# Second layer of an attention and two-FFN kernel: a larger room, a value's parts a stage later, banks in turn at two stages, one high part later

## The chip, the cores and the metric

The kernel runs on one core of a Trainium2 chip. The metric is device time in microseconds of one execution; times shown are medians of several. A profiled execution gives the trace that is quoted below. Engines are named as in the profile: PE is TensorE's matmuls, PEld its weight loads, DVE VectorE, ACT ScalarE, POOL GpSimd, SP SyncE, whose queue issues the loads and stores.

## The reference

What is computed, cut to what matters here: a thresholded attention, a gated layer, and a second layer whose activation is a square in the middle, zero below and the value itself above.

```python
def _moe_ref(x, w_gate, w_val, w_out):          # x: 2304 x 512, d_ff 1536
    gate = 1.0 / (1.0 + np.exp(-(x @ w_gate)))
    val = x @ w_val
    return (gate * val @ w_out).astype(np.float32)

def _moe2_ref(x, w_in, w_out):                  # d_ff 2048
    h = x @ w_in
    g = np.where(h >= 1, h, np.where(h <= -1, 0.0, (h + 1) ** 2 / 4.0))
    return (g @ w_out).astype(np.float32)

def reference(**kwargs):
    attn_out = _attn_ref(...)                   # 4 batches, 8 heads, 576 x 64
    x = attn_out.transpose(0, 2, 1, 3).reshape(2304, 512)
    return _moe2_ref(_moe_ref(x, ...), ...)
```

## The kernel before, in words

All matmuls are made of 32-bit floats split into a high and a low part: `hi` is ACT's copy of a value into the matmul's input type, `lo` is DVE's difference of the value and `hi`, and three matmuls (high by high, low by high, high by low) stand for one. So every operand of a matmul costs ACT one copy and DVE one difference, its "parts".

The program has three stretches. Attention comes first (to about 270 us), then most of the first layer. What the change touches is the third, from about 578 us: the last ten blocks of the first layer's last pass, and the second layer. Tokens are worked in three passes of 768 (`T`). The up-projection of two blocks of 128 hidden columns for one pass is a *stage*, `stage(g)`. It computes a two-by-two block product with seven products instead of eight: `product(i, ps)` issues six matmuls of 128x384 into one of two PSUM banks, `ps[0]` and `ps[1]`, and the table `PRODUCTS` says which. Products 0, 2, 4 and 6 use `ps[0]`, products 1, 3 and 5 `ps[1]`. ACT evacuates products 0 and 2 (`s1`, line 787, and `u2`, line 796), DVE makes five sums from the others (`add`, line 762), among them `u3`, which is the tile `high`. Their results are the two values `c[0]` and `c[1]` of the stage.

Stages 0 to 9 (`g` below `N1` = 10, `q = g - N1` negative) belong to the first layer, in pairs: an even stage gives two gates, an odd one the two values that are multiplied with them (`gated_steps`: the product on DVE, the high part on ACT, the low part on DVE). Stages 10 to 33 (`q` from 0 to 23) are the second layer, eight to a pass; `j` is the place in the pass, so stages 10, 18 and 26 are the first of a pass (`j` = 0), and 11, 19 and 27 the second. `value_steps` makes the activation there in four steps: the square on ACT (lines 683 and 684), the choice on DVE (690), the high part `hh` on ACT (692), the low part `hl` on DVE (693). `i` is 0 for a stage's first value and 1 for its second one.

Behind stage `g` TensorE issues output matmuls: `down` in the first layer (line 871), `down_pair(q - 1, y)` in the second (line 853), 36 matmuls of 128x512, 18 for the first value of the stage before and 18 for the second. After stages 0 and 8 none are issued; the lengths in `lens` say so with a 7.

The order on ACT and DVE is planned by hand-set due times. `due(first, last, steps)` puts a chain of steps on a list; each step has a time, an estimated cost on DVE and on ACT, and a mark that says whether it may stand between products (`small`). `fill(slot, room, act)` issues what is due: all whose `last` slot has come, and in order of time whatever still fits into the room. A stage has slots `4g` to `4g + 3`; the last one, behind its seven products, has the large room:

```python
                    room = lens[g] - 6.6 - (3 if j == 0 else 0)
                fill(4 * g + 3, room, room)
```

Between products, `fill(4 * g + 1, 2.6 if q == 0 else 1.5, 1.3, small=True)` stands behind product 1 and its sum, and small ones behind the later sums. The same list holds the parts of the weights (`split_steps`, lines 728 and 729: `win` for the next stage's products, `wout` for an output), the weights' differences (`w_sums`, line 633, into `tsum`), and the parts of the tokens for the next pass (`xflat`, `xmore`). Engines work their own queues in the order in which the program issues to them; SP loads weights (`load_pair`, `load_sums`) when the slots they go into are free. At a pass's second stage `store` copies the six finished output banks and issues their stores.

Of the kernel before, what the change touches and what calls it, by code (L numbers as in the profile page):

```python
# [13 lines left out]
AF = mybir.ActivationFunctionType  # L14
# [9 lines left out]
def f32(ap):  # L24

    return ap.bitcast(F32)
# [3 lines left out]
def kernel(  # L30
# [17 lines left out]
    nc = tc.nc  # L48
# [436 lines left out]
    def ffn(att):  # L485


        with ExitStack() as st:
# [170 lines left out]
            def load_sums(q):  # L659
                nc.sync.dma_start(out=tsum, in_=tsaved[q % NQ])  # L660
# [18 lines left out]
            def value_steps(c, r, h, at):  # L679


                def square():
                    nc.scalar.activation(r, c, AF.Relu, scale=0.5, bias=half)
                    nc.scalar.activation(r, r, AF.Square)

                return [
                    (at[0], 0, 1.6, False, square),
                    (
                        at[1], 0.84, 0, False,
                        lambda: nc.vector.scalar_tensor_tensor(c, c, 1.0, r, op0=ALU.max, op1=ALU.min),  # L690
                    ),
                    (at[2], 0, 0.72, False, lambda: nc.scalar.activation(h[0], c, AF.Copy)),
                    (at[3], 0.84, 0, True, lambda: nc.vector.tensor_tensor(h[1], c, f32(h[0]), op=ALU.subtract)),  # L693
                ]
# [5 lines left out]
            lens = [7] + [11] * (N1 - 3) + [7, 15] + [15] * (NPASS * NQ + 1)  # L700
            start = lambda g: sum(lens[:g])

            def due(first, last, steps):
                waiting.append((steps[0][0], len(order) + len(waiting), first, last, steps))
                waiting.sort(key=lambda x: x[:2])
# [33 lines left out]
            def due_w(g):  # L739
                at = start(g)  # L740
                sums = g < N1 + NQ
                if sums and g:
                    due(4 * g - 3, 4 * g - 1, [(at - 3 + 0.1 * i, 0.4, 0, True, w) for i, w in enumerate(w_sums(g))])
                for i, (when, first, last, cost) in enumerate(
                    ((-3.2 if sums else -1, 4 * g - 3, 4 * g - 1, 0.6), (1.3, 4 * g - 1, 4 * g + 1, 0.32), (1, 4 * g - 1, 4 * g - 1, 1.1))
                ):
                    due(first, last, split_steps(at + when, cost, cost - 0.1, *w_split(g, i)))

            def stage(g):

                q = g - N1
                n = q + N1 // 2 if q >= 0 else g // 2
                ps = [ps_a.tile([P, 512], F32, tag=f"a{i}", name="pu")[:, :HT] for i in range(2)]
                if q >= 0:
                    c = [(vals[:, 0], sqs[:, 1])[q % 2], (vals[:, 1], rbs, early_raw[1])[q % 3][:, :T]]
                elif g % 2 == 0:
                    c = cs[n] = [(sqs, vals)[n % 2][:, i] for i in range(2)]
                else:
                    c = [x[:, :T] for x in (rbs, early_raw[1])]
                s1, u2 = (hp_.tile([P, HT], F32, tag="act", name="act") for _ in range(2))  # L760
                u3 = high0[:, :HT]
                add = lambda o, a, b: nc.vector.tensor_tensor(o, a, b, op=ALU.add)  # L762
                t0, t1 = slice(0, HT), slice(HT, T)
                more, j = g + 1 < N1 + NPASS * NQ, (q % NQ if q >= 0 else g + NQ - N1)
                last, o = j == NQ - 1, (q // NQ + 1 if q >= 0 else 0)
                if more:
                    due_w(g + 1)
                if j == NQ - 4 and o < NPASS:
                    for i, w in enumerate(x_sums(o + 1)):
                        at = start(g + 1) + 8 * (i + 1) * lens[g] / 15  # L770
                        due(4 * g, 4 * (g + 3) - 1, [(at, 0.84, 0, True, w)])
                if last and more:
                    due_x(o + 1)
                for i in range(2):
                    if q >= 0:
                        first, end, at = 4 * g, 4 * g + 5, start(g + 1) + 5.2 + 0.3 * i
                        src = w32[q][i][:, KD * P : 2 * KD * P]
                    elif g % 2:
                        break
                    else:  # L780
                        f = F0 + 2 * n + i
                        wsp[0, NPASS - 1, f] = (None, None, *wout(n, i))
                        src = w32[0, NPASS - 1, f][:, 2 * KD * P :]
                        first, end, at = 4 * g, 4 * g + 7, start(g + 1) + 2 + 9 * i
                    due(first, end, split_steps(at, 0.6, 0.5, *wout(n, i), src))
                product(0, ps)
                nc.scalar.activation(s1, ps[0], AF.Copy)  # L787
                product(1, ps)
                add(c[0][:, t0], ps[1], s1)
                fill(4 * g + 1, 2.6 if q == 0 else 1.5, 1.3, small=True)  # L790
                if q + 1 >= NQ and more:
                    load_sums(q + 1)
                if q + 2 >= 0 and q + 2 < NPASS * NQ:
                    load_pair(q + 2)
                product(2, ps)
                nc.scalar.activation(u2, ps[0], AF.Copy)  # L796
                if lens[g] > 7 and q != 0:
                    fill(4 * g + 2, 0, 2.2, small=True, begin=True)
                product(3, ps)
                add(u3, ps[1], u2)  # L800
                fill(4 * g + 2, 0.45, 0, small=True)
                product(4, ps)
                add(c[1][:, t1], ps[0], u3)
                fill(4 * g + 2, 0.45, 0, small=True)
                product(5, ps)
                add(c[0][:, t1], ps[1], u2)
                fill(4 * g + 2, 0.45, 0, small=True)
                product(6, ps)
                add(c[1][:, t0], ps[0], u2)
                at = start(g + 1)  # L810
                if q < 0:
                    if g % 2 == 0:
                        sig = lambda x: nc.scalar.activation(x, x, AF.Sigmoid)
                        due(4 * g + 3, 4 * g + 7, [(at + 1.6 + i, 0, 0.9, True, lambda x=x: sig(x)) for i, x in enumerate(c)])
                    else:
                        for i in range(2):
                            h = hts[0, NPASS - 1, F0 + 2 * n + i] = h_tiles()
                            when = ((1.2, 1.3, 1.5), (1.25, 1.4, 1.7))[i]
                            if q == -1:
                                when = ((3.9, 4.2, 4.3), (6.5, 6.6, 7))[i]  # L820
                            due(4 * g + 3, 4 * g + 7, gated_steps(c[i], cs[n][i], h, [at + x for x in when]))
                    room = lens[g] - (4.6 if q == -1 else 5.6)
                else:
                    h = hts[q] = [h_tiles(), h_tiles()]
                    at += 7
                    for i in range(2):
                        r = vals[:, 1] if i and not more else sqs[:, 0]
                        if not more:
                            when = ((-6, -4, -3.8, -3.6), (-5, -3, -2.8, -2.6))[i]
                        elif last:  # L830
                            when = ((-2.5, -2.4, -2.2, -2), (1, 1.2, 1.4, 1.6))[i]
                        else:
                            when = ((-6.2, -6.15, -5.9, -5.5), (-5.4, -5.3, -5.2, -5.1))[i]
                        due(4 * g + 3, 4 * g + 7, value_steps(c[i], r, h[i], [at + x for x in when]))
                    room = lens[g] - 6.6 - (3 if j == 0 else 0)
                fill(4 * g + 3, room, room)

            def gated_steps(c, s, h, at):

                return [  # L840
                    (at[0], 0.92, 0, True, lambda: nc.vector.tensor_tensor(c, c, s, op=ALU.mult)),
                    (at[1], 0, 0.82, True, lambda: nc.scalar.activation(h[0], c, AF.Copy)),
                    (at[2], 0.92, 0, True, lambda: nc.vector.tensor_tensor(h[1], c, f32(h[0]), op=ALU.subtract)),
                ]

# [67 lines left out]
            early, taken, xops, begun, cs = {}, [], {}, [], {}  # L913
# [40 lines left out]
            n = 3 * KD * P  # L954
# [4 lines left out]
            for s in range(NB):  # L959
# [19 lines left out]
                if order[s][:2] == (0, 1) and later:  # L979
                    p, i, normalise = later.pop(0)  # L980
# [18 lines left out]
            for g in range(N1 + NPASS * NQ):  # L999
                q = g - N1  # L1000
# [3 lines left out]
                if q == -2:  # L1004
                    n = 2 * KD * P
# [3 lines left out]
                if q <= 0 < g != N1 - 2:  # L1009
                    n = NB - 2 + g  # L1010
# [61 lines left out]
```

## Time and profile before

| | |
|---|---|
| median of 3 runs | 1096.84 us (1093.95 to 1098.01) |
| the profiled execution | 1097.53 us, of which the span of its instructions is 1095.7 us |
| PE busy | 1075.7 us, 98% of the span |
| DVE busy | 898.3 us, 82% |
| ACT busy | 632.7 us, 58% |
| mean granted clock of TensorE | 0.995 of full |

The busy time of an engine is its share over stretches with different limits. For a change at single places, what counts is which engine waits there, for what, and how long; the chain that ended last and the timeline tell that.

### The profile page before, as it was taken

Reading aid. Unit: us, or ns where it says so; the run is one execution under the profiler, and the core shown is the slowest. Engines: PE = TensorE matmul, PEld = TensorE weight load, DVE = VectorE, ACT = ScalarE, POOL = GpSimd, SP = SyncE. Lnnn points to the kernel's source line nnn. Section 1 sums busy time; section 2 is a strip of 40 time slices with the busy share of each in tenths; the row PEclk is TensorE's granted clock in tenths of the full one; section 3 lists DMA queues with packets and bytes.
Section 4 is the critical chain, followed back from the end, with each engine's and each line's share of the span. In section 5 each row is a group of like instructions: output and inputs, shape, how many; then the busy total and the mean of one; then the engine's idle time right before and its main releaser. Section 6 shows DMA issues by size and latency. Waiting matters only on the chain.

```text
span 1095.7 us, 18519 instructions
## 1 busy us (share of the span) xinstructions
PE 1075.7 (98%) x6930; PEld 924.2 (84%) x6930; DVE 898.3 (82%) x1591; ACT 632.7 (58%) x1024; POOL 148.6 (14%) x311
## 2 busy tenths in 40 slices
PE   8999999999999999999999999999999999999998
PEld 6666666667999999999999999889888899889887
DVE  7999999997999999888797778977877667776663
ACT  6888888886434344333354544565566565665653
POOL 4556666562000000000000000000000000000000
PEclk9999999999999999999999999999999999999999
DMA  5344344514665566565541111222234322233301
GB/s 158 69 101 80 91 101 96 108 33 124 232 231 177 173 223 231 183 228 196 199 183 50 66 68 39 88 106 96 79 119 169 116 68 106 96 135 116 115 21 58
DMA packets 62842, 134.97 MB, mean 123 GB/s; under 512 B 9360, under 2 KB 35616, under 8 KB 62752
## 3 DMA queue, kind: packets, MB, share of 16 engines
q1 hardware_dynamic: 62608, 133.49, 38.1%
q8 instruction: 54, 0.88, 0.3%
q14 instruction: 36, 0.29, 0.1%
q10 hardware_dynamic: 144, 0.29, 0.1%
HBM read 106.96 MB, written 26.81 MB: 122 GB/s over the span
## 4 chain that ended last, share of the span: by engine, by line
PE 88%; ACT 5%; DVE 5%; issue 2%; POOL 0%; DVEq 0%; POOLq 0%
PE pu L674 22%; PE y L853 17%; PE y L871 13%; PE pgv L522 6%; PE pgv L521 6%; PE pgv L523 6%; PE av L339 6%; PE w L253 5%; PE w L307 4%; ACT ex L275 2%; PE w L250 1%; ACT xall L349 1%; DVE s L263 1%; DVE xflat L729 0%; ACT rl L325 0%
## 5 line engine op out<-in xcount | busy, mean ns | idle before, releaser
L853 PE MATMUL y<-wout,hh 128*128 128x512 f32 x576 | 186.3, 398 | 0.0
L674 PE MATMUL pu<-xflat,win 128*128 128x384 f32 x816 | 159.8, 337 | 1.8 <-DVE sqs L762 1.3
L674 PEld LDWEIGHTS pu<-xflat,win 128*128 128x128 f32 x816 | 143.5, 188 | 6.5 <-DVE sqs L762 2.3
L871 PE MATMUL y<-hh,wout 128*128 128x512 f32 (+1 forms) x576 | 146.2, 336 | 0.0
L522 PE MATMUL pgv<-xflat,win 128*128 128x384 f32 x400 | 133.9, 335 | 0.4 <-DVE xflat L514 0.4
L521 PE MATMUL pgv<-xflat,win 128*128 128x384 f32 x400 | 133.8, 335 | 0.0
L523 PE MATMUL pgv<-xflat,win 128*128 128x384 f32 x400 | 133.7, 334 | 0.0
L853 PEld LDWEIGHTS y<-wout,hh 128*128 128x128 f32 x576 | 109.6, 190 | 24.9
L674 PE MATMUL pu<-xmore,win 128*128 128x384 f32 x612 | 123.8, 336 | 1.4 <-ACT act L796 0.8
L263 DVE TENSOR_SCALAR_CACHE_REDUCE s<-w,nscale 128x576 f32<-128x576 f32 x144 | 112.4, 812 | 9.2 <-PE w L253 7.2
L853 PE MATMUL y<-wout,hl 128*128 128x512 f32 x288 | 115.2, 400 | 3.8 <-DVE hl L693 3.8
L283 DVE SCALAR_TENSOR_TENSOR p<-s,mx,ex 128x576 f32<-128x576 f32 x144 | 111.6, 808 | 0.0
L674 PEld LDWEIGHTS pu<-xmore,win 128*128 128x128 f32 x612 | 107.7, 188 | 3.4 <-ACT act L787 2.3
L275 ACT ACTIVATE ex<-s,mx 128x576 f32<-128x576 f32 x144 | 104.3, 766 | 6.2 <-DVE s L263 5.8
L871 PEld LDWEIGHTS y<-hh,wout 128*128 128x128 f32 x576 | 98.0, 188 | 11.3
L871 PE MATMUL y<-hl,wout 128*128 128x512 f32 (+1 forms) x288 | 97.1, 337 | 0.0
L266 POOL TENSOR_SCALAR mx<-mx,tau_b 128x1 f32<-128x1 f32 x144 | 87.5, 607 | 54.9 <-DVE s L263 54.6
L253 PE MATMUL w<-qk 64*128 64x288 f32 x512 | 89.9, 439 | 2.7 <-DVE s L263 2.7
L315 ACT ACTIVATE r<-w 128x1024 f32<-128x1024 f32 x64 | 65.2, 1018 | 30.3 <-PE w L307 29.9
L575 ACT ACTIVATE hh<-act 128x384 fp32r<-128x384 f32 x52 | 27.3, 524 | 93.0 <-DVE act L572 93.0
L253 PEld LDWEIGHTS w<-qk 64*128 64x128 f32 x512 | 50.8, 191 | 33.7 <-DVE s L263 18.4
L339 PE MATMUL av<-r,v 128*64 128x320 f32 (+1 forms) x512 | 75.8, 418 | 1.8 <-ACT xall L349 1.1
(164 smaller groups left out, 1903.8 us busy)
## 6 DMA issues: line engine op xcount, KB each, us to landing
words<-in_moe_w_out_dram SPq DMA_DIRECT2D x26, 512.0 KB
w<-saved SPq DMA_DIRECT2D x24, 512.0 KB
wmore<-saved SPq DMA_DIRECT2D x24, 512.0 KB
w<-saved SPq DMA_DIRECT2D x14, 768.0 KB
words<-in_moe_w_in_dram SPq DMA_DIRECT2D x16, 512.0 KB
saved<-w SPq DMA_DIRECT2D x16, 512.0 KB
tsum<-tsaved SPq DMA_DIRECT2D x16, 512.0 KB
wmore<-saved SPq DMA_DIRECT2D x10, 768.0 KB
```

Source lines behind the costliest of these rows:

```text
L253: nc.tensor.matmul(w[:, s, :HS], t[es, 0, u * P : u * P + P], t[es, 1, c], start=True, stop=True)
L263: nc.vector.tensor_scalar(t[:, e], w[:, :, :HS], nscale, None, op0=ALU.mult, op1=ALU.min, accum_out=mx[:, 0, e : e + 1])
L266: nc.gpsimd.tensor_scalar(mx[:, 1, e : e + 1], mx[:, 0, e : e + 1], tau_b, None, op0=ALU.add)
L275: nc.scalar.activation(ex[:, e], t[:, e], AF.Exp, scale=-1.0, bias=mx[:, 0, e : e + 1])
L283: nc.vector.scalar_tensor_tensor(pr[:, e], t[:, e].rearrange("p a b -> p (a b)"), mx[:, 1, e : e + 1], ex[:, e].rearrange("p a b -> p (a b ...
L339: nc.tensor.matmul(av[e * D : e * D + D, :n], vs[p % 3][:, e, c], rt[r][:, e, c] if c < nf else rl[r], start=c == 0, stop=c == nf,)
L521: nc.tensor.matmul(ps, ih[:, i, kk], xh, start=(kk == 0), stop=False)
L522: nc.tensor.matmul(ps, ih[:, i, kk], xl, start=False, stop=False)
L523: nc.tensor.matmul(ps, il[:, i, kk], xh, start=False, stop=(kk == KD - 1))
L674: nc.tensor.matmul(ps[bank], l[:, k], r[:, k], start=bool(new) and k == m == 0, stop=k == HK - 1 and m == 2, skip_group_check=True,)
L853: nc.tensor.matmul(y[b], l[:, ts_], r, start=first and m == 0, stop=last and m == 2)
L871: nc.tensor.matmul(at(y, a, b), l[:, ds_], r[:, c], start=new and m == 0, stop=last and m == 2, skip_group_check=True,)
```

## The change

Four edits, all in `stage` and in the steps it plans:

- Behind a stage of length 7 (so in stages 1 and 9) the two banks change roles.
- In stage 9 (`q == -1`) the high part of the second gated value is no longer marked as small, so it may not stand between products.
- In a pass's second stage (`j` = 1) the high and the low part of the second value get a chain of their own, which is due in the last slot of the stage behind.
- In a pass's first stage (`j` = 0) the last slot's room is reduced by 2 instead of 3.

```diff
@@ -751,6 +751,8 @@
                 q = g - N1
                 n = q + N1 // 2 if q >= 0 else g // 2
                 ps = [ps_a.tile([P, 512], F32, tag=f"a{i}", name="pu")[:, :HT] for i in range(2)]
+                if g and lens[g - 1] == 7:
+                    ps.reverse()
                 if q >= 0:
@@ -818,7 +820,7 @@
                             if q == -1:
                                 when = ((3.9, 4.2, 4.3), (6.5, 6.6, 7))[i]
-                            due(4 * g + 3, 4 * g + 7, gated_steps(c[i], cs[n][i], h, [at + x for x in when]))
+                            due(4 * g + 3, 4 * g + 7, gated_steps(c[i], cs[n][i], h, [at + x for x in when], q < -1 or i == 0))
                     room = lens[g] - (4.6 if q == -1 else 5.6)
@@ -831,15 +833,19 @@
-                        due(4 * g + 3, 4 * g + 7, value_steps(c[i], r, h[i], [at + x for x in when]))
-                    room = lens[g] - 6.6 - (3 if j == 0 else 0)
+                        steps = value_steps(c[i], r, h[i], [at + x for x in when])
+                        if j == i == 1:
+                            due(4 * g + 7, 4 * g + 7, steps[2:])
+                            steps = steps[:2]
+                        due(4 * g + 3, 4 * g + 7, steps)
+                    room = lens[g] - 6.6 - (2 if j == 0 else 0)
                 fill(4 * g + 3, room, room)
 
-            def gated_steps(c, s, h, at):
+            def gated_steps(c, s, h, at, small=True):
 
                 return [
                     (at[0], 0.92, 0, True, lambda: nc.vector.tensor_tensor(c, c, s, op=ALU.mult)),
-                    (at[1], 0, 0.82, True, lambda: nc.scalar.activation(h[0], c, AF.Copy)),
+                    (at[1], 0, 0.82, small, lambda: nc.scalar.activation(h[0], c, AF.Copy)),
```

The matmuls and their order stay as they are, apart from the banks of stages 1 and 9. ACT and DVE issue the same instructions in another order at four places: in stages 10 to 12, and at the ends of stages 18 and 26, which are alike. Three are shown, first before, then after; line numbers behind the first edit are larger by 2 to 8 in the changed kernel.

On DVE, the end of stage 18, the first of the second pass: the choice for the first value of the stage, the last weight parts for stage 19, the copies of three finished output banks (before L894, after L900), and the first sum of stage 19.

```order
L690 SCALAR_TENSOR_TENSOR vals<-vals,sqs 128x768
L729 TENSOR_TENSOR win_3507<-tsum,win_89 128x1024
L729 TENSOR_TENSOR win_3507<-w_2_84,win_89 128x256
L894 COPY xall<-y_3730 128x512
L894 COPY xall<-y_3732 128x512
L894 COPY xall<-y_3734 128x2x256
L762 TENSOR_TENSOR sqs<-pu,act 128x384
```

```order
L690 SCALAR_TENSOR_TENSOR vals<-vals,sqs 128x768
L729 TENSOR_TENSOR win_3507<-tsum,win_89 128x1024
L729 TENSOR_TENSOR win_3507<-w_2_84,win_89 128x256
L693 TENSOR_TENSOR hl<-vals,hh 128x768
L900 COPY xall<-y_3730 128x512
L900 COPY xall<-y_3732 128x512
L900 COPY xall<-y_3734 128x2x256
L764 TENSOR_TENSOR sqs<-pu,act 128x384
```

The low part of stage 18's first value now stands ahead of the copies; before, it stood behind stage 19's sums and a `wout` part. ACT's high part moves with it, from between stage 19's products to ahead of the last `win` part here.

On ACT, stage 10, the first of the second layer: the evacuation of product 0 (L787, after L789), that of product 2 (L796, after L798), the high part of stage 9's second gated value (`raw_88`, L842, after L848), and weight parts (L728).

```order
L787 ACTIVATE act<-pu 128x384
L842 ACTIVATE hh<-raw_88 128x768
L796 ACTIVATE act<-pu 128x384
L728 ACTIVATE win_89<-wmore 128x512
L683 ACTIVATE sqs<-vals,half 128x768
```

```order
L789 ACTIVATE act<-pu 128x384
L728 ACTIVATE win_89<-wmore 128x512
L728 ACTIVATE wout_3508<-w_1_83 128x512
L798 ACTIVATE act<-pu 128x384
L848 ACTIVATE hh<-raw_88 128x768
L683 ACTIVATE sqs<-vals,half 128x768
```

The high part has moved behind both evacuations, and two weight parts stand in its place. DVE's low part of that value moves behind the stage's five sums in the same way, a weight part takes its place there, and the second value's square and choice (L683, L684, L690) come into stage 10's end from stage 11's.

On ACT, from the end of stage 11, the second of the first pass, into stage 12: the square of stage 11's second value (`rb`), its high part (L692), and stage 12's evacuations of products 0 and 2.

```order
L683 ACTIVATE sqs<-rb,half 128x768
L684 ACTIVATE sqs<-sqs 128x768
L692 ACTIVATE hh<-rb 128x768
L787 ACTIVATE act<-pu 128x384
L728 ACTIVATE win_89<-w_1_83 128x512
L728 ACTIVATE wout_3508<-wmore 128x512
L796 ACTIVATE act<-pu 128x384
L728 ACTIVATE wout_6156<-w_0_82 128x512
```

```order
L683 ACTIVATE sqs<-rb,half 128x768
L684 ACTIVATE sqs<-sqs 128x768
L789 ACTIVATE act<-pu 128x384
L728 ACTIVATE win_89<-w_1_83 128x512
L728 ACTIVATE wout_3508<-wmore 128x512
L798 ACTIVATE act<-pu 128x384
L728 ACTIVATE wout_6156<-w_0_82 128x512
L692 ACTIVATE hh<-rb 128x768
```

The high part has moved behind stage 12's evacuations, and DVE's low part of it behind stage 12's sums.

## Rows read from the trace of the kernel before

**Rows 1.** Chain that ended last, second layer: start us, us, engine, line, count.

```profile
582.33 7.33 PE pu L674 x42
...
597.94 4.19 PE y L871 x24
...
840.24 7.38 PE pu L674 x42
849.72 9.88 PE y L853 x35
859.60 7.32 PE pu L674 x42
866.92 8.40 PE y L853 x36
...
979.58 9.86 PE y L853 x35
```

**Rows 2.** List of waits, PE: waited for; us in total, times, longest.

```profile
PE y L853 <- DVE hl L693: 3.8, 2, 1.9
```

**Rows 3.** Windows: us, busy PE PEld DVE ACT POOL, PEclk, DMA share, GB/s.

```profile
849.70:853.70 4.00, 3.98 (x11) 3.15 (x12) 2.35 (x3) 3.10 (x4) 0.00 (x0) 0.58 0.00 0
...
979.50:983.50 4.00, 3.92 (x10) 3.11 (x11) 2.35 (x4) 3.04 (x4) 0.00 (x0) 0.57 0.00 0
```

**Rows 4.** Timeline behind stage 19 and in stage 20, DVE and ACT: start, us.

```profile
848.72 0.95 DVE L693 TENSOR_TENSOR hl<-vals,hh 128x768 fp32r<-128x768 f32 x1
849.59 0.95 DVE L690 SCALAR_TENSOR_TENSOR raw<-raw,sqs 128x768 f32<-128x768 f32 x1
...
850.57 0.84 ACT L692 ACTIVATE hh<-raw 128x768 fp32r<-128x768 f32 x1 [3.70 <-DVE raw L690]
...
851.45 0.96 DVE L693 TENSOR_TENSOR hl<-raw,hh 128x768 fp32r<-128x768 f32 x1 [0.91 <-ACT hh L692]
...
861.79 0.56 DVE L762 TENSOR_TENSOR vals<-pu,act 128x384 f32<-128x384 f32 x1 [3.20 <-PE pu L674]
```

**Rows 5.** Timeline in stage 9, DVE.

```profile
680.47 0.95 DVE L611 TENSOR_TENSOR xall<-xall 128x768 f32<-128x768 f32 x1
681.93 0.56 DVE L762 TENSOR_TENSOR rb<-pu,act 128x384 f32<-128x384 f32 x1 [0.52 <-PE pu L674]
```

**Rows 6.** Timeline in stage 10, DVE and weight loads.

```profile
698.65 0.94 DVE L841 TENSOR_TENSOR raw<-raw,sqs 128x768 f32<-128x768 f32 x1
...
700.50 0.96 DVE L843 TENSOR_TENSOR hl<-raw,hh 128x768 fp32r<-128x768 f32 x1 [0.91 <-ACT hh L842]
...
700.90 1.00 PEld L674 LDWEIGHTS pu<-xmore,win 128*128 128x128 f32 x6 [1.12 <-ACT act L796]
...
701.72 0.55 DVE L762 TENSOR_TENSOR high<-pu,act 128x384 f32<-128x384 f32 x1
...
702.32 1.00 PEld L674 LDWEIGHTS pu<-xflat,win 128*128 128x128 f32 x6 [0.42 <-DVE high L762]
```

**Rows 7.** Groups by form, DVE, 700 to 760 us: busy us, mean ns.

```profile
L633 DVE TENSOR_TENSOR tsum<-wmore,tsum 128x256 f32<-128x256 f32 x5 | 2.1, 418 | 0.0
...
L729 DVE TENSOR_TENSOR win<-wmore,win 128x512 fp32r<-128x512 f32 x3 | 2.0, 681 | 0.0
```

**Rows 8.** Timeline in stage 12, ACT and weight loads.

```profile
729.92 0.85 ACT L692 ACTIVATE hh<-rb 128x768 fp32r<-128x768 f32 x1 [1.02 <-DVE rb L690]
...
731.19 0.99 PEld L674 LDWEIGHTS pu<-xmore,win 128*128 128x128 f32 x6 [0.76 <-ACT act L787]
...
732.88 0.99 PEld L674 LDWEIGHTS pu<-xflat,win 128*128 128x128 f32 x6 [0.69 <-DVE vals L762]
```

**Rows 9.** Windows of 1 us behind stage 19, columns as in rows 3.

```profile
849.00:850.00 1.00, 0.28 (x1) 0.28 (x2) 1.00 (x2) 0.00 (x0) 0.00 (x0) 1.00 0.02 8
```

**Rows 10.** Timeline behind stage 19, the parts of `tsum`.

```profile
853.02 1.04 ACT L728 ACTIVATE win<-tsum 128x1024 fp32r<-128x1024 f32 x1
...
854.10 1.23 DVE L729 TENSOR_TENSOR win<-tsum,win 128x1024 fp32r<-128x1024 f32 x1
```

## Prediction

> **What bounds the kernel now.** I read the chain that ended last first. In the second layer it is TensorE almost without a break: a stage of seven products takes 7.32 us, the 36 output matmuls behind it 8.40 us, and the next stage follows at once [rows 1]. So only a place where that chain is broken can give time back, and I looked for breaks by the starts of pieces: a stage that starts later than the end of the piece before it, or a piece that is too long for its count. Six places in reach of the change show one. The largest are in the second stage of the second and of the third pass: the seven products that start at 840.24 end at 847.62, the output matmuls go on at 849.72 and then need 9.88 us for 35, where 36 took 8.40 [rows 1]. The list of waits names the reason for the gap: `y` waited for `hl` of line 693, twice, 1.9 us the longest [rows 2]. The windows of these stretches show the rest: right behind each gap TensorE's granted clock is 0.58 and 0.57, a mixture of its two levels of 1.2 and 2.4 GHz, for some 4 us [rows 3]. Before the fall TensorE had idled; nothing else is different there.
>
> **The two pass starts (first value's parts before the stores).** In the order of before, the low part of the first value stands behind the next stage's seven products, two sums and a `wout` part: it runs at 848.72 and ends at 849.67 [rows 4], and the second matmul of the output waits for it. With the larger room it runs at the end of the first stage, some 9.5 us earlier, ahead of the copies of the stored tile. The DVE work is the same, one instruction of 0.95 us there and not here. From the start of the output (847.62) to the next stage (859.60) are 11.98 us; undisturbed it is 8.40 [rows 1]. The difference of 3.58 us is the stall and the slow clock together, and the second such place has the same piece, 9.86 us for 35 at 979.58 [rows 1]. Two of them: 7.16 us.
>
> What is late next? The second value's low part. Its chain at the same place is line 690 (849.59), the ACT copy (850.57), and line 693 (851.45, ended 852.41) [rows 4]. Without the first low part in front, all three come 0.87 us earlier (849.59 less 848.72), and the low part is ready at 851.54. The output reaches it after 18 of its 36 matmuls, at 847.62 + 4.20 = 851.82, and the low one is the second there. So it is in time by some 0.3 us, no more. The stage after that starts 3.6 us earlier than now; DVE idled 3.20 us before its first sum there (861.79, [rows 4]) and gains the 0.87, so it keeps pace with 0.5 us to spare. The copies of the stored tile begin 0.87 us later; nothing overwrites those banks until the next output, over 5 us on.
>
> **Banks in turn at two stages.** Stages 1 and 9 follow a stage without output matmuls between. Stages 0 and 1 take 15.61 us (582.33 to 597.94), two undisturbed stages 14.64 [rows 1]: 0.97 us lost, because product 0 writes the bank that product 6 just filled and DVE still reads. With the banks exchanged it writes the one freed a product earlier, and product 1 comes to the busy bank a product later, when that sum is over. I take 0.97 for stage 1. In stage 9 DVE stands in the way: the x sum (680.47) runs in front of the first sum, which idled 0.52 us for TensorE before 681.93 [rows 5]; it can come only that much earlier, and product 3 needs it. I take 0.52. The bound from below for both is 0, if DVE, full in the stages behind, starts its own chain no earlier; the bound from above is 0.97 each.
>
> The list of waits would give less for these places. It counts the idle time of matmuls, and the Trainium skill ("Perfetto Trace Analysis", "Identifying the Most-Contended Engine") says that matmul busy time misleads and the weight loads' is to be looked at. By matmul idle time the pass starts would be worth the 3.8 us of that row, not 7.16; the chain's starts and ends side with the skill.
>
> **One high part later (stage 10).** ACT copied the second gated value ahead of the evacuation of product 2, and waited with it for DVE's product at 698.65. So product 4 waited 1.12 us for that evacuation, and DVE waited 0.91 us for the copy before its low part at 700.50; the sum `high`, for which product 5 waits, ran at 701.72 [rows 6]. Afterwards a weight part of 512 and two differences of 256 stand there on DVE in place of the low part. By their means, 0.68 and 0.42 [rows 7], the sum starts at 698.65 + 0.94 + 0.68 + 2 x 0.42 = 701.11 or a little earlier. The evacuation no longer ends it, DVE does. Gain 0.6 to 0.7; I take 0.65. Bounds: 0, if another wait takes the place, and 1.54 (1.12 and the 0.42 that product 5 waits, [rows 6]). The value's own parts are needed only after 24 output matmuls, some 4 us after the stage, and come about 2 us before.
>
> **Second value's parts a stage later.** By the order it changes the first pass alone: at the other two the parts stood behind the next stage already. In stage 12 the weight loads of product 2 waited 0.76 us for the evacuation of product 0 and those of product 3 then 0.69 us for a sum; ACT's copy of that value, at 729.92, and DVE's low part behind it stood in front [rows 8]. Both go behind the stage's products, so 1.45 us at most; a little of it is caught up in the loads, and I take 1.4. It moves two instructions of 0.85 and 0.96 us to the end of stage 12, where the output needs them only after 18 matmuls (4.2 us). Two `wout` parts now run a stage later, so the load into their slot is issued some 6 us later on SP; that slot is read a stage on.
>
> **Sum.** 7.16 + 0.97 + 0.52 + 0.65 + 1.4 = 10.7 us. From the profiled execution's 1097.53 us that gives 1086.8. This execution lies 0.7 us above the median of the runs shown, so on the median it is 1086.1. I forecast 1086.5 us.
>
> **Rivals.**
> *Only the stalls come back, not the slow clock* (12 in 100). Of each 3.58 us the gap is 2.10 (847.62 to 849.72), so 1.48 is the clock. If the clock falls there for a reason other than the gap, or did not fall in the runs that are timed, 2.96 us are missing: 7.7 us gained, 1089.8. For it: the timed runs of before spread over 4 us, and one execution's trace can't tell how often the clock falls. Against: it fell behind both gaps [rows 3]. The Trainium skill ("TensorE: Matmul & The Clock Gate", "What's actually happening") says that the gate's watch on TensorE runs freely and isn't started by the kernel; by that, whether a short gap costs the clock would change from run to run, which is this rival, and two of two here neither show nor exclude it.
>
> *The second value takes over the wait* (10 in 100). Its low part is in time by 0.3 us. If DVE's queue slips, up to ACT's share of that chain, 0.91 us, shows at each pass start: 8.9 us gained, 1088.6; were the clock to fall again behind so short a gap, 2.96 us less, 1091.6, which I hold for unlikely, since stages 0 and 1 lost no more than the 0.97 us of their gap.
>
> *The stores collide with the loads* (10 in 100; 6 of them no change, 4 slower). The copies of the stored tile now start 0.87 us later, and behind the stores SP issues the load of `tsum` for the next stage. The transfers of that burst end by 849 [rows 9], so 849.9 afterwards. ACT reads `tsum` at 853.02, DVE finishes with it at 855.33 [rows 10]; both 0.87 earlier afterwards, and TensorE needs the result in product 2 of the next stage, at about 858.1 (859.60 less 3.58, and two of seven products). So the burst may end 2.2 us later before ACT waits, and 5.8 us later, at 855.7, before TensorE does. Past that, x us of lateness cost twice x + 1.48. The whole gain is gone at x = 3.9, with the burst ending at 859.6, and the kernel is 0.5% slower (5.5 us) from x = 6.6, at 862.3; with x = 7 it would be 1103. Against: the engines are idle again at 849, and nothing adds bytes.
>
> **How the numbers follow.** 68 in 100 for the forecast; its own range by the bounds above is 1085 to 1089. The range that should hold 8 in 10 takes in the first two rivals, and the spread of the runs: 1083.5 to 1091.5. About 0.5% is what a measurement here can tell from no change, so faster means below 1091.4. The forecast and the second rival lie there, the first mostly, with some risk from the spread: faster 0.87, same 0.09, slower 0.04.
>
> **What would show it.** The rows of waits for `hl` gone and the clock at 1.00 in the second stage of each pass, with 36 output matmuls in 8.4 us; stages 0 and 1 in 14.7 us; stage 10 still with a short wait for the sum `high`, but none for the evacuation of product 2; stage 12 without a wait. It is wrong if `y` waits for `hl` again half an output later, if the clock still drops there, or if DVE idles for `tsum`.

## The result, and the profile after

The changed kernel takes 1086.1 us (median of 5 runs, 1086.05 to 1087.43), before 1096.84 us (5 runs, 1093.93 to 1098.25): a ratio of 0.991, interval 0.990 to 0.993. The forecast was 1086.5 us. The profiled execution has a span of 1084.3 us; PE is busy for 1070.0 us of it (99%), DVE for 898.2, ACT for 634.1, and the mean granted clock is 1.000 in place of 0.995; of the falls behind the 0.995, two stand at the places of [rows 3] and one in the attention (0.50 from 12 to 14 us).

The chain that ended last, changed kernel, the pieces that answer to [rows 1] (start, us, engine and line, count):

```profile
581.22 14.66 PE pu L674 x84
...
669.52 14.93 PE pu L674 x84
...
701.27 8.38 PE y L877 x48
709.65 7.35 PE pu L674 x42
...
732.63 8.40 PE y L859 x36
...
835.58 7.37 PE pu L674 x42
842.95 8.31 PE y L859 x36
851.26 7.35 PE pu L674 x42
...
962.12 7.37 PE pu L674 x42
969.49 8.31 PE y L859 x36
977.79 7.35 PE pu L674 x42
```

Read it by the distance from one start to a later one. Stage 19's start to stage 20's was 19.36 us (840.24 to 859.60, [rows 1]) and is 15.68 (835.58 to 851.26): 3.68 us less. The third pass gives 3.64 (19.31 to 15.67). Stages 0 and 1 need 14.66 us for 84 matmuls, 0.95 less. The windows of both output stretches of the changed kernel, columns as in [rows 3]:

```profile
842.90:851.20 8.30, 8.30 (x38) 6.75 (x37) 6.46 (x8) 6.01 (x8) 0.00 (x0) 1.00 0.36 129
969.40:977.70 8.30, 8.30 (x38) 6.75 (x37) 6.45 (x8) 5.98 (x8) 0.00 (x0) 1.00 0.37 123
```

PE is busy throughout and the clock stays at its upper level. In PE's list of waits no `hl` of line 693 is left in the second layer; this is the whole list there:

```profile
PE pu L674 <- DVE high L764: 0.4, 1, 0.4
```

DVE at the second pass's second stage, which answers to [rows 4]:

```profile
834.40 0.95 DVE L693 TENSOR_TENSOR hl<-vals,hh 128x768 fp32r<-128x768 f32 x1
835.26 1.88 DVE L900 COPY xall<-y 128x512 f32<-128x512 f32 x3
...
844.06 0.95 DVE L690 SCALAR_TENSOR_TENSOR raw<-raw,sqs 128x768 f32<-128x768 f32 x1
845.93 0.96 DVE L693 TENSOR_TENSOR hl<-raw,hh 128x768 fp32r<-128x768 f32 x1 [0.92 <-ACT hh L692]
```

The first value's low part ends some 7.6 us before the output starts at 842.95. The second one's ends at 846.89, and the output reaches it at about 842.95 + 4.20 = 847.15: in time, and not by much.

### The profile page after: what moved, and what is told of

It reads as the page before. It is cut to its first block, busy times and chain, and to the rows that moved or that the text cites. A ratio compares the mean times of both kernels' runs of the same rounds, so it can differ in the third digit from the quotient of the medians.

```text
span 1084.3 us, 18520 instructions
## 1 busy us (share of the span) xinstructions
PE 1070.0 (99%) x6930; PEld 921.4 (85%) x6930; DVE 898.2 (83%) x1591; ACT 634.1 (58%) x1024; POOL 149.1 (14%) x311
## 4 chain that ended last, share of the span: by engine, by line
PE 88%; DVE 5%; ACT 4%; issue 2%; POOL 0%; DVEq 0%; POOLq 0%
PE pu L674 22%; PE y L859 17%; PE y L877 13%; PE pgv L522 6%; PE pgv L521 6%; PE pgv L523 6%; PE av L339 6%; PE w L253 5%; PE w L307 4%; ACT ex L275 2%; PE w L250 2%; DVE xflat L729 1%; DVE s L263 1%; ACT xall L349 1%; DVE win L729 1%
## 5 line engine op out<-in xcount | busy, mean ns | idle before, releaser
L859 PE MATMUL y<-wout,hh 128*128 128x512 f32 x576 | 184.0, 394 | 0.0
L253 PE MATMUL w<-qk 64*128 64x288 f32 x512 | 87.7, 430 | 3.2 <-DVE s L263 3.2
```

The costliest lines, as they stand in the source:

```text
L253: nc.tensor.matmul(w[:, s, :HS], t[es, 0, u * P : u * P + P], t[es, 1, c], start=True, stop=True)
L859: nc.tensor.matmul(y[b], l[:, ts_], r, start=first and m == 0, stop=last and m == 2)
```

## The experiments

Times are medians, ratios are against the kernel before on the same chip. A *pass start* is the second stage of the second or third pass with its output, where the gap was. "Lost" is the length of such a stretch less that of the changed kernel.

**1. Without the larger room.**

```diff
-                    room = lens[g] - 6.6 - (2 if j == 0 else 0)
+                    room = lens[g] - 6.6 - (3 if j == 0 else 0)
```

> The change without its larger room: banks in turn, one high part later and second value's parts later stay. Theory (each pass start costs its gap and then a slow clock): both pass starts keep a gap of 2.1 us and lose 3.6 to 3.7 us each, so 1086.1 + 7.3 = 1093.4 us, and the granted clock is near 0.58 for some 4 us behind both gaps. Rival (only the stall belongs to the gap, the clock falls for another reason or in a part of the executions): 36 output matmuls take 8.4 us beside a gap of 2.1 in some executions, so times between 1090.3 and 1093.4 us, and the mean clock of the timed runs differs from run to run by up to 0.003.

1091.47 us (0.996, 0.995 to 0.997). The profiled execution, the longest of the five at 1093.74 us, lost 3.68 us at each start, with PE waiting 1.88 us for `hl` there and 35 matmuls in 9.86 us behind it. Three other runs lie at 1091.26 to 1091.47 us, 2.3 us below, at a mean clock of 0.998 in place of 0.997. These runs have no trace; their mean clock leaves room for one fall in the whole execution (experiment 2), so at least one of their two gaps went without. That speaks for the rival.

**2. Before, unchanged, for the clock of each run.**

> The kernel before, unchanged, for the granted clock of each timed run. If both pass starts fall to the slow clock in every execution, its mean clock is 0.995 in all runs, within 0.001, and the spread of 4 us comes from elsewhere. If the clock falls there in a part of the executions, runs near 1094 us have a mean clock 0.001 to 0.003 higher than runs near 1098 us, because one or two falls of some 4 us at about 0.58 are 0.0015 to 0.003 of the span.

1095.55 us (11 runs, 1094.94 to 1096.77). Its trace decides more than the times. The chain of this execution, behind the two gaps, each again with a wait of 1.88 us:

```profile
849.58 9.88 PE y L853 x35
859.46 7.32 PE pu L674 x42
...
979.45 8.32 PE y L853 x35
987.76 7.35 PE pu L674 x42
```

Its windows there:

```profile
850.00:852.00 2.00, 2.00 (x6) 1.52 (x6) 1.09 (x2) 1.57 (x2) 0.00 (x0) 0.50 0.00 0
...
980.00:982.00 2.00, 2.00 (x10) 1.62 (x9) 1.08 (x2) 1.68 (x3) 0.00 (x0) 1.00 0.00 0
```

Same kernel, same gap, same work: behind the first the clock is at 1.2 GHz and 35 matmuls take 9.88 us, behind the second it stays at 2.4 and they take 8.32. Over the 50 runs of the kernel before in these experiments whose clock is listed, 23 have a mean clock of 0.998 and take 1095.20 us on average, 13 have 0.997 (1096.06) and 14 have 0.994 or 0.995 (1096.59). None is above 0.998; of ten runs of the changed kernel four are at 0.999 or 1.000. Part of before's spread is the clock. But a mean clock doesn't say where it fell. In the traces 0.998 is one fall, 0.997 two and 0.995 three, and in seven of the 14 traces, of kernels with and without gaps, one of them stands in the first 16 us of the attention (experiment 12).

**3. Gaps of two other lengths.** On the kernel of experiment 1 the low part is written in two pieces at the first start (128 and 640 columns) and twice at the second.

```diff
+                        if i == 0 and q == 8:
...
+                                for s in (slice(0, P), slice(P, T)):
+                                    nc.vector.tensor_tensor(h[1][:, s], c[:, s], f32(h[0])[:, s], op=ALU.subtract)
...
+                        if i == 0 and q == 16:
...
+                                nc.vector.tensor_tensor(h[1], c, f32(h[0]), op=ALU.subtract)
+                                lo()
```

> The change without its larger room, with gaps of two other lengths: at the first pass start the low part is written in two pieces of 128 and 640 columns, so that the output matmuls wait some 1.4 us in place of 2.1; at the second it is written twice, so that they wait some 3.05 us. Theory (a gap of this size brings the slow clock, with a fixed cost of about 1.5 us): 1.4 + 1.5 = 2.9 us lost at the first, 3.05 + 1.5 = 4.55 at the second, granted clock near 0.58 behind both. Rival (the slow time grows with the gap): 1.4 + 1.0 and 3.05 + 2.2. Rival (the clock falls by chance): one of the two pieces shows no slow clock at all, most likely the one behind the shorter gap.

1091.73 us. The chain of this kernel at both starts:

```profile
844.11 8.35 PE y L877 x35
852.46 7.35 PE pu L674 x42
...
973.72 9.88 PE y L877 x35
983.60 7.35 PE pu L674 x42
```

PE waited 1.22 us at the first and lost 1.49 us in all, with no fall of the clock: there the theory missed, and the piece behind the shorter gap came as the second rival said. PE waited 2.87 us at the second and lost 4.65; the 35 matmuls there are as slow as behind 1.88 us. So, where it comes, the slow clock costs 1.56 us behind either gap (9.88 less the 8.32 of experiment 2); the rival by which it grows with the gap is out.

**4. The second value's low part late.** On the changed kernel it is written twice at the first start, and twice and a half time more at the second.

```diff
+                        if i == 1 and q in (8, 16):
...
+                            def twice(lo=lo, n=q // 16 * 384, c=c[i], h=h[i]):
+                                nc.vector.tensor_tensor(h[1], c, f32(h[0]), op=ALU.subtract)
+                                if n:
+                                    nc.vector.tensor_tensor(h[1][:, :n], c[:, :n], f32(h[0])[:, :n], op=ALU.subtract)
+                                lo()
```

> The change, with the low part of the second value late at the two pass starts: it is written twice at the first, and twice and a half time more at the second (0.95 and 1.5 us more on VectorE). The margin of the changed kernel is about 0.26 us by its trace (the part ends at 846.89, the output reaches it at about 847.15), so the output matmuls should break in their middle for 0.7 us and 1.25 us. Theory (any gap brings the slow clock): 0.7 + 1.5 and 1.25 + 1.5, 1086.1 + 4.95 = 1091.0 us. Rival (short gaps cost themselves alone): 0.7 + 1.25, 1088.0 us, granted clock 1.0. If the margin is larger than worked out, both gaps are shorter by the same amount.

1088.47 us (0.993, 0.992 to 0.995); the one run at a clock of 1.000 took 1087.94. The chain at the first start, and the two ends of the low part at the second:

```profile
846.51 0.97 DVE hl L841
...
847.51 0.97 DVE hl L693
...
848.52 4.16 PE y L869 x17
852.68 7.35 PE pu L674 x42
...
973.62 0.97 DVE hl L841
...
975.21 0.97 DVE hl L693
```

836.16 to 852.68 is 16.52 us, 0.84 lost for a last writing that starts 1.00 us later (846.51 to 847.51); the second start lost 1.44 (17.11 us) for 1.59 (973.62 to 975.21). So the margin of the changed kernel is about 0.15 us at both. Behind PE's waits of 0.56 and 1.14 us the clock stayed up, as the rival had it.

**5. Many gaps.** High and low part of the first value behind the next stage's products at all stages of a pass but the last.

```diff
-                        if j == i == 1:
+                        if j == i == 1 or i == 0 and not last:
```

> The change, with the high and the low part of the first value moved behind the next stage's products at all stages but the last of a pass, so that the output matmuls of some 20 stages wait for the low part. Each place is one more throw for the clock. Theory A (a gap of 1.9 us always brings the slow clock): every piece of 35 output matmuls takes 9.87 us. Theory B (the fall needs a gap and comes in a part of the cases, those gaps that meet a watch which runs on its own): pieces of either 8.3 or 9.87 us, both kinds present behind gaps of one length, 5 of 6 slow if the six gaps of 1.88 us seen so far are typical; shorter gaps (0.56 to 1.22 us) showed none. Theory C (some other condition of the place decides): all stages of one kind agree, and the two pass starts differ from the others.

1152.63 us (1.052, 1.050 to 1.054). Four neighbours of its chain:

```profile
870.43 9.88 PE y L859 x35
...
889.73 8.42 PE y L859 x35
...
907.58 9.87 PE y L859 x35
...
926.89 8.44 PE y L859 x35
```

The waits that end there, from the timeline (idle time before in brackets):

```profile
907.58 0.50 PE L859 MATMUL y<-wout,hl 128*128 128x512 f32 x1 [1.88 <-DVE hl L693]
926.89 0.50 PE L859 MATMUL y<-wout,hl 128*128 128x512 f32 x1 [1.88 <-DVE hl L693]
```

And its windows, ahead of and behind two of them:

```profile
905.00:907.50 2.50, 0.70 (x4) 0.32 (x2) 2.02 (x5) 2.36 (x3) 0.00 (x0) 1.00 0.00 0
907.60:911.60 4.00, 4.00 (x11) 3.15 (x12) 3.22 (x4) 2.70 (x5) 0.00 (x0) 0.62 0.26 49
...
924.30:926.80 2.50, 0.71 (x4) 0.33 (x2) 2.02 (x5) 2.34 (x3) 0.00 (x0) 1.00 0.00 0
926.90:930.90 4.00, 4.00 (x17) 3.27 (x18) 3.23 (x4) 2.69 (x5) 0.00 (x0) 1.00 0.23 60
```

What TensorE did ahead of the two is alike; behind one the clock falls, behind the next it doesn't. Of 17 gaps of 1.88 us in this trace 8 are followed by the slow clock and 9 aren't; 2.48 us and twice 3.62 us are, 1.28, 0.50 and 0.49 us aren't. So theories A and C are out, and of theory B it holds that the fall comes in a part of the cases, in 8 of 17 rather than 5 of 6. It doesn't look like throws of a coin: from 870.43 us on, all twelve gaps of 1.88 us take turns, slow and fast. A fall doesn't simply spare the next gap, though: the falls behind 2.48 us (720.52) and 1.88 us (739.84) follow each other, and the next two gaps (759.27, 777.06) both went without. No run here tells what picks.

**6. Without the second value's parts later.**

```diff
-                        if j == i == 1:
-                            due(4 * g + 7, 4 * g + 7, steps[2:])
-                            steps = steps[:2]
```

> The change without the second value's parts a stage later; the larger room, the banks and the high part stay. By the order the parts then stand in front of the next stage's evacuations at all three pass starts (stages 12, 20 and 28), because the larger room lets them in at the other two. Theory (each such place costs what stage 12 cost in the kernel before, 1.3 us): 3 x 1.3, so 1086.1 + 3.9 = 1090.0 us. Rival (only stage 12 had the wait, as the prediction's sum has it): 1087.4 us.

1089.59 us (0.994, 0.993 to 0.996). Stage 11's start to the end of stage 12 takes 22.98 us, as in the changed kernel: no wait in stage 12. But stages 19 and 20 need 24.37 us to the end in place of 23.03, and stages 27 and 28 24.36: 1.33 us lost at each. Neither expectation came: three places were expected or one, and it was two, without the one of the prediction.

**7. The larger room alone, on the kernel before.**

```diff
-                    room = lens[g] - 6.6 - (3 if j == 0 else 0)
+                    room = lens[g] - 6.6 - (2 if j == 0 else 0)
```

> The kernel before with the larger room alone. Theory drawn from the runs so far (the room mends both pass starts and, by letting more of stage 10's second value into that stage's end, the wait of stage 12 as well, but puts the second value's parts in front of stages 20 and 28, where each costs 1.34 us): 36 output matmuls in 8.3 to 8.4 us at both pass starts, stage 12 without a wait, stages 20 and 28 with waits of 1.3 us each, so by the pieces 4.2 us of gaps, 1.5 us for each fall of the clock that goes, and 1.3 at stage 12 less 2.7: 2.8 us faster at least, 5.9 where both falls go. Rival (as the prediction added it, the terms are independent): 7.2 us faster, stage 12 still with its wait and stages 20 and 28 without one.

1091.21 us (0.996, 0.995 to 0.997), 4.55 us below the runs of before beside it, as the first theory had it. Both pass starts are without a gap, and stage 11's start to stage 12's end takes 22.99 us in place of 24.29. In stage 12 the first evacuation now waits for TensorE and not for the high part in front of it, and stage 20's weight loads wait as stage 12's did in [rows 8]:

```profile
729.46 0.49 ACT L787 ACTIVATE act<-pu 128x384 f32<-128x384 f32 x1 [0.88 <-PE pu L674]
...
856.76 0.99 PEld L674 LDWEIGHTS pu<-xmore,win 128*128 128x128 f32 x6 [0.76 <-ACT act L787]
858.44 1.00 PEld L674 LDWEIGHTS pu<-xflat,win 128*128 128x128 f32 x6 [0.69 <-DVE vals L762]
```

**8. The second value's parts later alone, on the kernel before.**

```diff
+                        if j == i == 1:
+                            due(4 * g + 7, 4 * g + 7, steps[2:])
+                            steps = steps[:2]
```

> The kernel before with the second value's parts a stage later alone. Theory: by the order nothing moves but the two instructions at stage 12, its waits of 0.76 and 0.69 us go and the piece of stages 11 and 12 is 1.3 us shorter; gaps of 1.88 us stay at both pass starts. The time is 1.3 us below that of before, less than the spread of before's runs, so the piece tells. Rival: the two instructions are late for the output behind stage 12 and it breaks there.

1095.52 us (11 runs; 0.999, 0.998 to 1.000): not to be told from before by its time, as expected. The same stretch takes 22.93 us (713.03 to 735.96), 1.36 less than before. At its pass starts the first gap of 1.88 us went without a fall and the second with one: 2.08 and 3.64 us lost. The former is the price of the stall alone.

**9. Without the high part later, and 10. without the banks in turn.**

```diff
-                            due(4 * g + 3, 4 * g + 7, gated_steps(c[i], cs[n][i], h, [at + x for x in when], q < -1 or i == 0))
+                            due(4 * g + 3, 4 * g + 7, gated_steps(c[i], cs[n][i], h, [at + x for x in when]))
```

```diff
-                if g and lens[g - 1] == 7:
-                    ps.reverse()
```

> The change without the high part later in stage 10. Theory: product 4 waits for the evacuation of product 2 again, 0.65 to 0.8 us lost, 1086.8 us. Rival (the weight part that stands in its place on VectorE costs as much): no difference, 1086.1 us.

> The change without the banks in turn at stages 1 and 9. Theory: stages 0 and 1 take 15.6 us again and stages 8 and 9 15.5, so 0.95 + 0.6 more, 1087.65 us. Rival: VectorE, full behind stage 9, gives the second half back, and only 0.95 shows: 1087.05 us.

Without the high part later: 1087.27 us. From stage 0's start to the output behind stage 10 are 120.76 us, with it 120.05 (581.22 to 701.27 above), so 0.71 lost, and the wait of 1.12 us for `act` is back. Without the banks: 1089.0 us (1087.96 to 1089.11; 1087.96 at a clock of 1.000). Stages 0 and 1 lose 0.92 us and stages 8 to 10 0.71; to the last output it is 1.68. VectorE didn't give the second half back. The median is 1.35 us above the theory's time; the four runs other than the profiled one have mean clocks of 0.996 to 0.998 and no trace, so the pieces give the price here, not the median.

**11. Less between the products of stage 10.** The changed kernel's one large wait in the second layer, 0.67 us of the weight loads for `high`, has a weight part and two differences ahead of the sum:

```profile
698.92 1.00 PEld L674 LDWEIGHTS pu<-xflat,win 128*128 128x128 f32 x6 [0.67 <-DVE high L764]
```

```diff
-                fill(4 * g + 1, 2.6 if q == 0 else 1.5, 1.3, small=True)
+                fill(4 * g + 1, 1.5, 1.3, small=True)
```

> The change with a smaller room between the products of stage 10 (1.5 in place of 2.6): a weight part and one difference that stood on VectorE ahead of the sum for which product 5 waits go behind it. Theory (that wait of 0.67 us is all that is left there): the sum starts when product 3 ends, some 0.8 us earlier, stage 10 has no wait, 1086.1 - 0.65 = 1085.45 us. Rival (the weight part is late for stage 11, or the value's low part for the output): 1086.1 us or up to 0.7 more.

1085.69 us (0.991, 0.989 to 0.992). The timeline of stage 10 there:

```profile
698.63 0.56 DVE L764 TENSOR_TENSOR high<-pu,act 128x384 f32<-128x384 f32 x1 [0.29 <-PE pu L674]
...
699.24 1.05 PEld L674 LDWEIGHTS pu<-xflat,win 128*128 128x128 f32 x6
```

The sum now waits for PE and product 5's loads wait for nothing; from stage 0's start to the output behind stage 10 it is 119.46 us, 0.59 less. Two runs at a clock of 1.000 took 1085.05 and 1085.17 us, two of the changed kernel 1086.05 and 1086.10. The gain at the place is shown; in the totals the intervals overlap.

**12. The changed kernel again.**

> The changed kernel again, on the same chip as the runs beside it. No gap over 0.4 us at the pass starts, so no fall of the clock there in any execution; runs at a mean clock of 1.0 near 1086.1 us. Against before the ratio depends on how often the clock falls in before: with two falls at the pass starts 11 us faster, with one 9.5, with none 7.9, each less or more by the 1 to 1.5 us by which the attention differs between executions.

1086.64 us (0.992, 0.990 to 0.993), no run at a clock of 1.000, 9.1 us below the runs of before beside it; the two outputs at the pass starts take 8.31 us each. In all seven traces of kernels with the larger room and the normal low part, none of the 14 pass starts has a gap or a slow clock. Mean clocks of 1.0 were expected and didn't come, and the trace shows where the clock fell instead: in the attention. The same stretch of it in this execution and in the one of the result, columns as in [rows 3]:

```profile
12.00:14.00 2.00, 2.00 (x23) 1.42 (x20) 1.91 (x7) 0.04 (x1) 0.97 (x4) 0.50 1.02 363
...
12.00:14.00 2.00, 2.00 (x16) 1.43 (x16) 2.00 (x5) 2.00 (x4) 1.07 (x2) 1.00 1.06 384
```

So the mean clock of a run counts a fall that no edit touches.

## Why the prediction was right, point by point

**Pass starts** (7.16 predicted): 3.68 + 3.64 = 7.32 us between the two traces; the output there takes 8.31 us undisturbed, not the 8.40 that the term set against it. The stall alone is 2.08 us (experiment 8), as the prediction split it (2.10); the clock is 1.56, predicted 1.48. What the row of 3.8 us in the list of waits misses is therefore mostly the slow clock behind the gaps; the prediction put it to matmul busy time as a measure. But the term took the profiled execution for the rule, in which the clock fell behind both gaps. Over all traces it fell behind 14 of 25 gaps of 1.88 us, so by that share (an estimate, since 17 of the 25 are from experiment 5) a start costs 2.08 us and in a bit over half of the cases 1.56 more, 2.95 on average. The mechanism of the first rival is thus partly real: in the second layer every fall stood behind a gap of 1.88 us or more, and a gap of 1.88 us didn't ensure one. What it was to cost was out: of the 2.96 us at stake about 1.7 come back on average. The median of before's runs beside the result, 1096.84 us, lay high; over the 50 listed runs it is 1095.71, over ten of the changed kernel 1086.4, a gain of 9.3 us. So it is luck that the sum of 10.7 us, with both falls counted in full, met the difference of 10.74 between the two medians; the time of 1086.8 us that the sum gives from the profiled execution stands on firmer ground, since that execution had both falls. By the Trainium skill ("TensorE: Matmul & The Clock Gate", "What's actually happening") the gate's watch runs freely; experiment 5, 8 of 17 behind like gaps, fits that, though no run here shows the watch itself.

**Second value takes over the wait**: didn't happen; the margin of 0.3 us was 0.15 (experiment 4), and the waits of 0.56 and 1.14 us past it brought no fall of the clock. **Stores against loads**: no sign, PE has no wait behind the stores.

**Banks** (0.97 and 0.52): 0.95 and 0.62 between the traces, 0.92 and 0.71 taken away.

**High part** (0.65): 0.71 taken away. As predicted, the evacuation no longer ends that wait, a shorter one for `high` does.

**Second value's parts later** (1.4): here the step failed that said "by the order it changes the first pass alone". Stage 12 did get 1.31 us shorter, but the room does that as well (experiments 6 and 7): ACT's high part then ends (at 728.58 in experiment 7) before product 0 of stage 12 is there to be evacuated at 729.46, even with the high part in front. What the edit does beside the room is to hold the second value's parts back at stages 20 and 28, where the room would bring them forward and cost 1.33 us each. The sum came out because 1.3 us at stage 12 is counted once either way; each edit's share was wrong. The order of the changed kernel against that of before could not show it, only that of each edit alone.

**Sum**: 10.7 predicted. Between the two traces the terms add up to 11.0 (7.32 + 0.95 + 0.62 + 0.81 for stage 10 + 1.31); the attention, which no edit touches, was 1.1 us shorter in the execution after (stage 0 at 581.22, before at 582.33). From stage 0's start to the last output's the whole is 10.37 us shorter (492.86 to 482.49): the stretches between the places that were summed came out 0.64 us longer together, which the sum didn't foresee.

## What to carry to other kernels

A piece of the chain that is too long for its count is worth more than the idle row names: here 2.08 us of stall brought 1.56 us of slow clock with it, behind about half of the gaps, so such a term needs its frequency from several traces before it is multiplied. Edits to a planner's room and due times aren't independent: build each alone and compare its order before their terms are added. Where a value is ready just in time, lengthen it on purpose once: what was added, less the time that the chain then loses, is the margin.

## What the runs showed of the hardware

Behind gaps of one length in the second layer, 1.88 us, TensorE's granted clock fell to 1.2 GHz in 14 of 25 cases and stayed at 2.4 in 11, with like work ahead of them (busy for 0.70 and 0.71 of 2.5 us at two neighbours); behind 2.48 us and more it fell in 4 of 4, behind 1.28 us and less in none of 6. At the pass starts each fall cost 1.56 us, behind 2.87 us as behind 1.88. What decides between two like gaps stays open; in the one trace with many of them they took turns.

The length of a single wait isn't the whole of it: in the first 16 us of the attention the clock fell in 7 of 14 traces, where no wait of TensorE's matmuls from 5 us on was longer than 0.92 us. Executions of one program also differ by up to 1.2 us ahead of stage 0 (581.22 us in the result's trace, 582.39 in experiment 12's). That arises in the first 20 us: the first twelve matmuls of line 253 take 2.21 us in the one and 3.53 in the other, whose clock then falls as well. What makes the one or the other start stays open.
